# A new order of all steps in a planned block-sparse attention and cosine MLP kernel

## The chip, the cores and the metric

The kernel runs on one core of one Trainium2 chip. The metric is the device time of a launch in microseconds (us), lower is better. A launch was timed in three runs, and one execution was profiled.

## The reference: what is computed

Four batches of eight heads, 768 positions and a head dimension of 64 go through attention with a block mask: blocks of 32, a window of one block to each side, the first and last blocks as rows and columns, and three sampled blocks for each row of blocks. The result, 3072 tokens of 512 values, goes through an MLP with a cosine gate.

```python
scores = scale * np.matmul(q, k.transpose(0, 1, 3, 2))
mask = np.abs(blk_i - blk_j) <= window
mask = mask | (blk_i == 0) | (blk_j == 0) | (blk_i == n_blocks - 1) | (blk_j == n_blocks - 1)
... sampled blocks are set in mask
attn = softmax(np.where(mask, scores, -1e9))
x = np.matmul(attn, v), heads side by side, (3072, 512)
h = x @ w_in                     # (3072, 2048), weights in float64
out = (h * np.cos(h)) @ w_out    # (3072, 512)
```

## The kernel before, in words

Values are split into a high and a low float16 half, so each product is three matmuls. The work is cut into **tiles** of 128 query rows. A batch has five sparse tiles (numbers 0 to 4, then 6 to 10 and so on) and one dense tile with the first and last blocks (5, 11, 17, 23), 24 in all. A sparse tile is worked in four **units** of two heads over 352 gathered keys, a dense one in eight units of one head over 768 keys, 112 units in all.

A unit goes through these steps, named in the planner as given in brackets: scores on TensorE (`qk`, lines 1509 to 1540) into the one scores buffer `sp`; mask and maximum on VectorE (`mx`, 1553); exponential on ScalarE (`ex`, 1575); cast to float16 (`ph`, ScalarE, 1585) and the rest by subtraction (`pl`, VectorE, 1589) into one of three `ring` buffers; a transposing transfer from SP's queue (`PT`, 1604) into one of three `PT` buffers; and the product with the values on TensorE (`pv`, 1614, 1626, 1640) into `xp`. After the last unit the tile is normalised (1653 to 1666) and its output transposed by another transfer (`xT`, 1669). Values come from a scratch tensor into one of two `V` buffers: plain loads from SP (`vg`, 1478 to 1486) and four indirect gathers by GpSimd (`vi`, 1492). One of these two buffers holds the sampled indices and constants at first. Keys are split per batch, transposed into the one `W` (1360) and gathered into `Wg` (1366).

Two tiles make one **feed-forward** pass, 12 in all, each of four chunks of 512 inner columns: four up blocks of 12 matmuls (`m`, 1801), copied out by ScalarE (1810), then rounding, cosine, products and split on VectorE and ScalarE (1820 to 1842), and four down blocks of 6 matmuls (`d`, 1851). Four `g` buffers and two `hs` buffers carry the chunks. At the start 32 float64 weight chunks are loaded (`wl`, 1704), converted with integer operations on VectorE (1712 to 1716), scaled and split; the last eight of them land in `g` buffers.

The order is worked out by a planner before anything is issued. `plan_kernel` (line 523) lists 3193 steps with an engine, a cost, a position, and the buffers read, written and taken. `Plan.run` (398) simulates the engines and repeatedly issues the step that can begin first; among those within `DELTA` = 0.038 us the one of lowest position. Buffers of a class are handed out in the order of the positions of their first steps. The result is one fixed sequence per engine; each engine works it through in order, waiting where data are late. A transfer from SP is modelled as one queue, `dma_free` (lines 492 to 502): it begins 0.65 us after an issue time `hw` or when the queue is free, lasts its `dma` figure (1.73 us for a probability transpose with `hw` 0.63), and counts as landed `DMA_DONE` = 1.15 us later. GpSimd's gathers are booked on the same queue for 1.5 us each (504). A position is a formula of some hundred parameters (`PARAMS`) plus up to three entries of a table `NUDGES`, found by the step's name.

Of the kernel before, what the change touches and what calls it, by code (L numbers as in the profile page):

```python
# [56 lines left out]
NUDGES = dict(  # L57
    idx=3.61, sx=-0.42, regs=-2.95, regs0=-8.34, regs0_0=-6.69, regs1=6.82, regs1_0=-17.04, regs2=3.29, regs2_0=-20.5, regs0_1=-6.69, const=-17.11,
    kload=-0.63, kload0=-0.87, kload0_0=-10.62, ksq=9.39, ksq0=-7.31, ksq0_0=-21.27, kload0_1=-7.01, ksq0_1=-41.01, kload0_2=-66.32, ksq0_2=11.5,
    kred=-0.92, kall=1.38, kall0=-31.15, ksc=-0.19, ksc0=-12.07, regs3=21.51, regs3_0=25.08, regs4=9.54, regs4_0=-19.9, regs1_1=-20.28, regs2_1=3.97,  # L60
    regs3_1=-8.55, regs4_1=15.17, vload=9.28, vload0=-15.15, vload0_0=11.52, vsq=-6.11, vsq0=13.32, vsq0_0=4.72, vload0_1=2.59, vsq0_1=-3.92,
    vload0_2=38.86, vsq0_2=14.54, vred=42.82, vred0=3.99, vall=1, vall0=-0.62, vsc=-5.56, vsc0=-4.67, ql=-0.06, ql0=11.94, qsq=-0.33, qsq0=17.87,
    qsc=-3.82, qsc0=1.9, qu=0.12, qnu=-14.73, qnu0=-6.95, qhi=2.68, qlo=2.81, qlo0=1.37, uT=-0.62, uT0=-18.36, up=2.32, up0=11.32, khi=4.75,
    khi0=9.03, klo=14.9, klo0=12.03, kT=-0.1, kT0=-22.55, kT0_2=4.55, kp=4.16, kp0=0.97, kp0_2=2.55, kT0_3=-0.33, kp0_3=6.32, kT0_4=22.41,
    kp0_4=39.57, kT0_5=6.88, kp0_5=4.01, vhi=0.82, vhi0=13.51, vhi0_0=0.77, vlo=6.66, vlo0=-1.79, vlo0_0=32.44, vst=10.44, vst0=38.45, vst0_0=-44.56,
    vhi0_1=-13.35, vlo0_1=34.43, vst0_1=-3.14, vlo0_2=0.6, vst0_2=29, vhi0_3=4.95, vlo0_3=9.17, vst0_3=-0.45, vhi0_4=-0.81, vst0_4=-36.52,
    vhi0_5=3.24, vlo0_5=22.52, vst0_5=5.35, vg=2.22, vg0=-25.12, vg0_0=11.42, vg0_1=3.7, vg0_2=-0.77, vi=-2.42, vi0=-1.84, vi0_0=-2.26, vi0_1=-10.33,
    vi0_2=9.28, vi0_3=23.96, wgd=-0.98, wgd0=-12.88, wga=3.36, wga0=1.25, wl=-2.63, wl0=-13.24, wc=-1.9, wc0=-0.7, wc0_0=8.57, wc0_1=-15.78,
    wc0_2=-17.45, wsq=-0.65, wsq0=-1.13, wl1=6.28, wc1=13.61, wc1_0=9.36, wc1_1=-9.88, wc1_2=-12.47, wsq1=13.17, wl2=-47.49, wl3=-7.45, wc3=3.57,
    wc3_0=1.61, wc3_1=-6.76, wc3_2=-5.03, wsq3=-6.1, wred=-2, wred0=2.15, wall=1.32, wall0=6.84, wsc=-15.18, wsc0=-20.51, whi=-6.02, whi0=1.04,  # L70
    wlo=2.63, wlo0=3.59, whi2=-0.92, wlo2=-0.14, wl4=9.77, wl5=0.82, wc5=-3.55, wc5_0=20.27, wc5_1=-20.07, wc5_2=-5.13, wsq5=28.26, wl6=8.99,
    wl7=-4.71, wc7=-3.29, wc7_0=-4.88, wc7_1=24.05, wc7_2=9.52, wsq7=-27.78, wred4=-0.63, wall4=0.94, wsc4=-5.92, whi4=18.59, wlo4=7.34, whi6=17.59,
    wlo6=6.23, wl8=-23.81, wl9=6.85, wc9=-14.69, wc9_0=-18.76, wc9_1=21.47, wc9_2=-8.03, wsq9=0.29, wl10=-3.72, wl11=14.55, wc11=-15.06, wc11_0=1.46,
    wc11_1=2.59, wc11_2=6.74, wsq11=16.26, wred8=1.1, wall8=-5.89, wsc8=16.58, whi8=31.98, wlo8=-1.44, whi10=-20.53, wlo10=5.79, wl12=4.39,
    wl13=-15.45, wc13=8.94, wc13_0=-0.92, wc13_1=-0.6, wc13_2=-14.42, wsq13=1.15, wl14=-4.43, wc14=-8.3, wc14_0=-6.73, wc14_1=-8.72, wc14_2=5.6,
    wl15=13.82, wc15_0=10.16, wc15_1=-9.19, wc15_2=0.79, wsq15=5.99, wred12=-0.61, wall12=6.43, wsc12=15.17, whi12=3.82, wlo12=0.5, whi14=49.08,
    wlo14=5.47, wl16=13.24, wl17=30.85, wc17=0.85, wc17_0=-17.27, wc17_1=-0.03, wc17_2=1.79, wsq17=-4.22, wl18=22.91, wc18=-4.52, wc18_0=-2.64,
    wc18_1=-4.76, wc18_2=4.91, wsq18=10.95, wl19=7.23, wc19=-4.21, wc19_0=6.85, wc19_2=-10.01, wsq19=2.09, wred16=-8.69, wall16=17.87, wsc16=-24.31,
    whi16=2.21, wlo16=-18.87, whi18=35.39, wlo18=-19.16, wl20=14.49, wl21=-41.89, wc21=5.55, wc21_0=-1.63, wc21_1=-9.78, wc21_2=-18.56, wsq21=-23.09,
    wl22=50.3, wl23=6.87, wc23=-3.56, wc23_0=-24.76, wc23_1=-9.51, wc23_2=-16.68, wsq23=-11.56, wred20=-30.93, wall20=-3.44, wsc20=-0.04,  # L80
    whi20=-15.71, wlo20=-15.74, whi22=-6.83, wlo22=10.13, wl24=-2.43, wc24=6.19, wc24_0=-3.62, wc24_2=-0.46, wsq24=16.72, wl25=5, wc25=-0.46,
    wc25_0=1.55, wc25_1=0.25, wc25_2=-1.23, wsq25=4.27, wl26=11.94, wc26=-8.12, wc26_0=-16.55, wc26_1=-1.96, wc26_2=-11.56, wsq26=7.92, wl27=0.35,
    wc27=-3.37, wc27_0=-5.24, wc27_1=5.68, wc27_2=49.47, wsq27=4.91, wred24=-15.24, wsc24=-0.49, whi24=-4.49, wlo24=-9.29, whi25=1.62, wlo25=19.32,
    whi26=33.15, wlo26=-4.66, wl28=-8.97, wc28=5.55, wc28_0=-0.52, wc28_1=0.13, wsq28=-6.28, wl29=-1.2, wc29=-61.45, wc29_0=5.2, wc29_1=7.84,
    wc29_2=-31.01, wsq29=-38.92, wl30=8.34, wc30=-9.45, wc30_0=12.37, wc30_1=31.8, wc30_2=20.24, wsq30=0.34, wl31=14.98, wc31=-0.21, wc31_0=-6.47,
    wc31_1=5, wc31_2=-2.32, wsq31=26.29, wred28=4.21, wsc28=5.26, whi28=-19.62, wlo28=-6.21, whi30=2, wlo30=0.25, wmax=15.33, ql1=-5.72, qsq1=-14.68,
    qsc1=3.98, qnu1=1.34, qhi1=-47.08, qlo1=-6.38, uT1=-18.81, up1=-3.53, vg1=-17.37, vg1_0=-9.27, vg1_2=0.1, vi1=30.91, vi1_0=0.48, vi1_1=-18.54,
    vi1_2=0.12, vi1_3=0.12, qk=-0.17, qk0=-58.98, qk0_0=0.24, mx=0.27, mx0=-2.49, mx0_0=-21.81, nb=-3.59, nb0=-8.96, nb0_0=2.59, ex=1.35, ex0=-3.07,
    ex0_0=-22.48, ph=-3.63, ph0=-21.88, ph0_0=-4.4, pl=-21.9, pl0=-22.66, pl0_0=-3.74, PT=-0.26, PT0=4.89, PT0_0=-4.28, pv=0.3, pv0_0=-5.56,
    qk0_1=0.86, mx0_1=-11.94, nb0_1=2.39, ex0_1=2.98, ph0_1=-5.55, pl0_1=15.27, PT0_1=-2.63, pv0_1=6.05, qk0_2=7, mx0_2=-13.62, nb0_2=7.03,  # L90
    ph0_2=0.14, pl0_2=-16.04, PT0_2=-3.48, pv0_2=15.14, qk0_3=18.43, mx0_3=-9.04, nb0_3=9.8, ex0_3=-3.71, ph0_3=7.63, pl0_3=-9.05, PT0_3=-7.28,
    pv0_3=-3, rs=-2.94, rs0=-31.95, rr=-6.44, rr0=6.78, no=0.17, no0=-18.12, xh=0.87, xh0=12.96, xl=0.07, xl0=-4.32, xT=-3.02, xT0=12.24, xp=-14.84,
    xp0=4.93, wgd1=-25.62, wga1=-4.93, ql2=3.86, qsq2=0.31, qsc2=-12.49, qu2=10.26, qnu2=7, qhi2=-4.29, qlo2=-24.12, uT2=-4.61, up2=0.35, vg2=-4.52,
    vg2_0=-58.49, vg2_1=-15.91, vg2_2=-6.89, vi2=-7, vi2_0=-17.32, vi2_1=-0.54, vi2_2=-18.18, vi2_3=2.73, qk1=-0.39, qk1_0=-16.06, mx1=-5.68,
    mx1_0=-7.63, nb1=0.27, nb1_0=0.17, ex1=11.47, ex1_0=4.98, ph1=-9.02, ph1_0=0.22, pl1=-6.66, pl1_0=-0.96, PT1=-13.96, PT1_0=-15.61, pv1=10.71,
    pv1_0=-16.09, qk1_1=-4.02, mx1_1=-2.64, nb1_1=-3.56, ex1_1=16.53, ph1_1=-3.84, pl1_1=-6.4, PT1_1=0.59, pv1_1=1.72, qk1_2=-2.71, mx1_2=1.47,
    nb1_2=0.13, ex1_2=11.37, ph1_2=-4.64, pl1_2=-1.25, PT1_2=-4.99, pv1_2=9.69, qk1_3=-1.21, mx1_3=1.13, ex1_3=-6.56, ph1_3=3.94, pl1_3=-2.83,
    PT1_3=2.29, pv1_3=13.9, rs1=-2.68, rr1=5.45, no1=-7.24, xh1=-3.98, xl1=-9.69, xT1=25.61, wgd2=-13.96, wga2=-2.4, m=0.34, m0=7.68, m0_0=-2.33,
    turn=-7.57, turn0=-18.26, turn0_0=1.62, ev=-4.58, ev0=-4.52, ev0_0=-21.06, sce=-7.02, sce0=50.11, ka=5.66, ka0=1.78, ka0_0=-3.5, kb=-1.13,
    kb0=4.68, kb0_0=-13.36, sin=0.46, sin0=-0.93, sin0_0=2.79, gm=1.05, gm0=-7.53, gm0_0=24.9, gh=-2.94, gh0=21.43, gh0_0=-12.51, gl=-17.79,  # L100
    gl0=-5.58, gl0_0=-4.21, turn0_1=5.61, ev0_1=0.45, sce1=1.82, ka0_1=-9.91, kb0_1=-14, sin0_1=1.7, gm0_1=14.55, gh0_1=-7.7, gl0_1=-13.54,
    m0_2=-3.6, turn0_2=-40.38, ev0_2=2.87, sce2=1.57, ka0_2=4.5, kb0_2=-6.01, sin0_2=5.35, gm0_2=1.98, gh0_2=-6.52, gl0_2=11.76, m0_3=-3.22,
    turn0_3=16.55, ev0_3=11.54, sce3=4.59, ka0_3=8.66, kb0_3=3.09, sin0_3=-1.35, gm0_3=16.12, gh0_3=-10.16, gl0_3=-6.97, d0=-3.17, d0_0=-3.86,
    o=1.98, o0=-0.17, o0_0=8.97, o0_1=11.85, d0_1=3.25, d0_2=1.64, d0_3=2.26, st=16.31, st0=-13.05, st0_0=5.76, st0_1=16.22, ql3=14.11, qsq3=10.1,
# [1825 lines left out]
```

## Time and profile before

| | |
|---|---|
| median of 3 runs | 895.02 us (893.42 to 896.33) |
| span of the profiled execution | 851.5 us |
| that execution's own time | not listed |
| instructions in the span | 23033 |
| mean granted TensorE clock | 0.936 |
| TensorE busy with matmuls | 727.7 us, 9272 matmuls |
| VectorE, ScalarE, GpSimd busy | 644.8, 624.8, 101.8 us |

The span runs from the first to the last instruction on the core; the time of a launch also holds what lies around it. Busy times of engines overlap one another. A granted clock of 1.0 is 2.4 GHz and 0.5 is 1.2 GHz. "DMA" is the mean busy share of the core's 16 transfer engines; it can pass 1.0 where packets of two queues overlap.

### The profile page before, as it was taken

The page shows a single profiled execution, that of the slowest core. Times are in us where ns is not written, and L with a number is a line of the kernel's source. Part 1 is how long each engine was busy: PE and PEld are TensorE (multiplying, and loading weights), DVE is VectorE, ACT ScalarE, POOL GpSimd, SP SyncE. Part 2 cuts the span into 40 slices and gives each one's busy share as a digit, 9 for nine tenths or more (in the row PEclk, how much of TensorE's full clock was granted, in tenths as well). Part 3 has the DMA queues.
Part 4 walks back from the last instruction along what each step waited for, and adds up shares of the span by engine and source line. Part 5 has one row for each costly group of instructions (what it writes and reads, how often), then busy time and mean ns, then how long its engine had stood idle before and what let it go on. Part 6 is the DMA issues. An engine that isn't in the chain of part 4 may idle for free.

```text
span 851.5 us, 23033 instructions
## 1 busy us (share of the span) xinstructions
PE 727.7 (85%) x9272; PEld 506.8 (60%) x9272; DVE 644.8 (76%) x1632; ACT 624.8 (73%) x1193; POOL 101.8 (12%) x128
## 2 busy tenths in 40 slices
PE   3556667779999869987999979999988869999997
PEld 2444554546767537656767548677665548576583
DVE  3999989998967776878668876879578746867352
ACT  1686846888867898788758978779669857769342
POOL 5211231000030101200020111000020111000000
PEclk9965697879999979999999999999999989999999
DMA  9999893398895989899979999989696997855300
GB/s 253 324 208 275 211 264 98 73 233 166 213 222 127 201 164 194 157 230 149 228 159 182 196 177 170 216 133 165 191 156 116 184 196 155 181 83 118 87 2 25
DMA packets 313306, 146.54 MB, mean 172 GB/s; under 512 B 266224, under 2 KB 290928, under 8 KB 313200
## 3 DMA queue, kind: packets, MB, share of 16 engines
q1 hardware_dynamic: 308080, 129.35, 73.1%
q0 software_dynamic: 5120, 15.73, 8.4%
q8 instruction: 72, 1.18, 0.6%
q14 instruction: 34, 0.28, 0.1%
HBM read 68.23 MB, written 12.58 MB: 95 GB/s over the span
## 4 chain that ended last, share of the span: by engine, by line
PE 40%; ACT 12%; DMA 11%; DVE 10%; issue 3%; SPq 1%; DVEq 0%; ACTq 0%
PE ph L1801 19%; PE po L1851 15%; DMA PT<-ring 6%; ACT P L1575 4%; DVE P L1553 3%; DMA W<-kn 2%; DMA xT<-n 2%; ACT ring L1585 2%; DVE ring L1589 1%; PE xp L1640 1%; PE xp L1626 1%; PE sp L1520 1%; DVE hs L1833 1%; DVE g L1842 1%; DVE g L1824 1%
## 5 line engine op out<-in xcount | busy, mean ns | idle before, releaser
L1801 PE MATMUL ph<-xT,w 128*128 128x256 f16 x2304 | 270.8, 278 | 10.1 <-DMA xT<-n 6.7
L1851 PE MATMUL po<-w,g 128*128 128x512 f16 x1152 | 269.0, 383 | 8.6 <-ACT g L1839 7.1
L1801 PEld LDWEIGHTS <-w 128*128 128x128 f16 x2304 | 226.5, 99 | 47.6 <-issue 7.3
L1851 PEld LDWEIGHTS <-g 128*128 128x128 f16 x1152 | 108.2, 98 | 128.0 <-ACT g L1839 7.4
L1575 ACT ACTIVATE P<-P,sm 128x352 f32<-128x352 f32 (+1 forms) x224 | 151.9, 679 | 28.8 <-DVE sm L1570 19.3
L1492 POOL DMA_INDIRECT V<-scr,gidx x80 | 89.2, 1115 | 613.4 <-PE xp L1614 316.0
L1589 DVE TENSOR_TENSOR ring<-P,ring 128x704 f16<-128x704 f32 (+1 forms) x112 | 100.1, 906 | 31.5 <-ACT ring L1585 30.1
L1810 ACT ACTIVATE hs<-ph,sm 128x512 f32<-128x512 f32 x96 | 64.4, 680 | 50.8 <-PE ph L1801 42.8
L1585 ACT CAST ring<-P 128x704 f16<-128x704 f32 (+1 forms) x112 | 86.5, 785 | 13.0 <-DMA PT<-ring 11.9
L1553 DVE CUSTOM_DVE_ANT_1 P<-sp,bias 128x352 f32<-128x352 f32 x160 | 77.7, 518 | 14.1 <-PE sp L1526 13.1
L1833 DVE SCALAR_TENSOR_TENSOR hs<-hs,sm,g 128x1024 f32<-128x1024 f32 x48 | 61.0, 1281 | 23.6 <-ACT g L1828 22.4
L1520 PE MATMUL sp<-W,U 128*128 128x192 f16 x320 | 53.2, 268 | 29.2 <-DVE sm L1553 27.7
L1828 ACT ACTIVATE g<-g,sm 128x1024 f32<-128x1024 f32 x48 | 54.7, 1146 | 23.7 <-DVE g L1824 23.4
L1842 DVE TENSOR_TENSOR g<-hs,g 128x1024 f16<-128x1024 f32 x48 | 58.6, 1223 | 17.1 <-ACT g L1839 16.9
L1839 ACT ACTIVATE g<-hs 128x1024 f16<-128x1024 f32 x48 | 50.4, 1051 | 18.2 <-DVE hs L1833 17.5
L1824 DVE SCALAR_TENSOR_TENSOR g<-g,hs 128x1024 f32<-128x1024 f32 x48 | 58.3, 1220 | 0.5
L1521 PEld LDWEIGHTS <-U 128*128 128x128 f16 x320 | 33.4, 104 | 35.7 <-issue 32.0
L1614 PE MATMUL xp<-V,PT 96*32 96x64 f16 x1920 | 31.0, 202 | 22.0 <-DMA PT<-ring 18.8
L1820 DVE TENSOR_SCALAR g<-hs 128x1024 f32<-128x1024 f32 x48 | 32.9, 691 | 21.8 <-ACT hs L1810 20.1
L1521 PE MATMUL sp<-W,U 128*128 128x64 f16 x320 | 48.7, 207 | 0.0
L1626 PE MATMUL xp<-V,PT 128*128 128x64 f16 x960 | 45.5, 201 | 0.0
L1614 PEld LDWEIGHTS <-PT 96*32 96x32 f16 x1920 | 21.6, 102 | 37.7 <-DMA PT<-ring 25.9
(176 smaller groups left out, 896.0 us busy)
## 6 DMA issues: line engine op xcount, KB each, us to landing
V<-scr SPq DMA_DIRECT2D x20, 384.0 KB
stage<-in_k_dram SPq DMA_DIRECT2D x12, 512.0 KB
w<-in_moe_w_in_dram SPq DMA_DIRECT2D x12, 512.0 KB
w<-in_moe_w_out_dram SPq DMA_DIRECT2D x12, 512.0 KB
V<-scr SPq DMA_DIRECT2D x8, 768.0 KB
scr<-n SPq DMA_DIRECT2D x21, 256.0 KB
qs<-in_q_dram SPq DMA_DIRECT2D x20, 256.0 KB
U<-U SPq DMA_DIRECT2D x40, 128.0 KB
```

Of the source, the lines that this page charges most:

```text
L1492: self.nc.gpsimd.indirect_dma_start(V[:96, 2 + j, :], None, self.scr[b][:, :], bass.IndirectOffsetOnAxis(ap=self.gidx[:96, c : c + 1], axi ...
L1521: mm(spv[:, :, 96:128].rearrange("p y (n c) -> p y n c", c=hf), u, ends, start=False, stop=False)
L1553: self.nc.vector.tensor_tensor_reduce(out=self.p_view(n, Pt)[:, a].rearrange("p (n c) -> p n c", c=hf), in0=sp[:, :w].rearrange("p (n c) - ...
L1575: self.nc.scalar.activation(Pv[:, a], Pv[:, a], AF.Exp, scale=qc[:, 4:5], bias=nb[:, bcol : bcol + 1], accum_out=sums[:, 2 * j + a : 2 * j ...
L1585: self.nc.scalar.copy(R[:, :, 0, : self.width(n)], self.p_view(n, Pt))
L1589: self.nc.vector.tensor_tensor(R[:, :, 1, :w], self.p_view(n, Pt), R[:, :, 0, :w], ALU.subtract)
L1801: self.nc.tensor.matmul(ph[:, ff, :], self.W1[p][:, wl, cc, c * P : (c + 1) * P], xT[:, xl * NCC + cc, :], start=(j == 0), stop=(j == len( ...
L1810: self.nc.scalar.activation(hs[:, h * 512 : h * 512 + 512], ph.rearrange("p f t -> p (f t)"), AF.Copy, scale=self.turns[b][:, p : p + 1])
L1824: self.nc.vector.scalar_tensor_tensor(kt, kt, MAGIC, hs, op0=ALU.subtract, op1=ALU.subtract)
L1833: self.nc.vector.scalar_tensor_tensor(hs, hs, c[:, p : p + 1], kt, op0=ALU.mult, op1=ALU.mult)
L1842: self.nc.vector.tensor_tensor(g[:, 1024:2048], hs, g[:, 0:1024], ALU.subtract)
L1851: self.nc.tensor.matmul(po, g[:, gl, ff, t * P : (t + 1) * P], self.W2[p][:, wl, ff, :], start=(first and ff == half * hf and j == 0), sto ...
```

## The change

`NUDGES` is removed. A list `POS` of 3193 numbers takes its place, and each step's position is the entry with its own number, whatever the formula gave. The planner's model of transfers is changed: SP's queue and GpSimd's queue each have an end of their own, transfers that overlap run at half speed while they do, the figure of an SP transfer is multiplied by 1.1, a gather takes 1.1 us, and landing comes 1.3 us after the end. `PARAMS`, the steps and their engines, and every function that issues an instruction stay.

```diff
-NUDGES = dict(
-    idx=3.61, sx=-0.42, regs=-2.95, regs0=-8.34, regs0_0=-6.69, regs1=6.82, regs1_0=-17.04, regs2=3.29, regs2_0=-20.5, regs0_1=-6.69, const=-17.11,
...
+POS = [
+    -532.03, -810.177, 89.397, -131.085, -65.302, -89.144, -544.854, -540.202, -322.968, -385.34, -105.865, -127.653, -505.194, -345.924, -499.035,
...
-DMA_DONE = 1.15
+DMA_DONE = 1.3
+DMA_SLOW = 1.1
+POOL_DMA = 1.1
...
+class Queues:
+    def __init__(self):
+        self.ends = [0.0, 0.0]
+
+    def run(self, which, at, work):
+        other = self.ends[1 - which]
+        begin = max(at, self.ends[which])
+        if other <= begin:
+            end = begin + work
+        else:
+            shared = other - begin
+            end = begin + 2 * work if work <= shared * 0.5 else begin + shared + (work - shared * 0.5)
+            self.ends[1 - which] += (min(end, other) - begin) * 0.5
+        self.ends[which] = end
+        return end
...
-        for key in nudge_keys(name):
-            o.pos += NUDGES.get(key, 0.0)
+        if len(self.ops) < len(POS):
+            o.pos = POS[len(self.ops)]
...
-                dma_free = d + o.dma
-                o.done = dma_free + DMA_DONE + o.lat
+                o.done = dma.run(0, h + 0.65, o.dma * DMA_SLOW) + DMA_DONE + o.lat
             elif o.dma:
-                dma_free = max(o.end + 1.0, dma_free) + o.dma
-                o.done = dma_free + DMA_DONE + o.lat
+                o.done = dma.run(1, o.end + 1.0, POOL_DMA) + DMA_DONE + o.lat
```

Because buffers are handed out by position, the two lists of positions give the order in which steps take them. The scores buffer, `xp`, `Wg`, `qs` and `P` go out in the same order but for the key and value maxima of one batch; the others change among neighbours:

| buffer | before | after |
|---|---|---|
| `V`, first four | index tile, tile 0, tile 2, tile 1 | index tile, tile 1, tile 0, tile 2 |
| `g`, weight chunks | 24, 27, 28, 25, 29, 26, two of pass 0, 30, 31 | 31, 25, 24, 29, 27, 26, 28, one of pass 0, 30 |
| `ring`, tiles 7 to 9 | 7_0 7_1 7_2 8_0 7_3 8_1 9_0 8_2 8_3 9_1 | 7_0 7_1 7_2 7_3 8_0 8_1 8_2 8_3 9_0 9_2 |
| `ring`, tiles 14 to 17 | 14_0 14_1 15_1 14_2 15_2 15_0 14_3 16_0 15_3 16_1 16_2 17_0 16_3 | 14_0 14_1 14_3 14_2 15_0 15_3 15_2 15_1 16_1 16_0 16_2 16_3 17_0 |
| `ring`, tiles 19 to 23 | 20_1 ahead of 19_3; 22_3 ahead of 23_0 | 19_3 ahead of tile 20; 23_0 ahead of 22_3 |

## Rows read from the trace of the kernel before

**Rows 1.** The page's line of engines: busy us, share of the span, instructions.

```profile
PE 727.7 (85%) x9272; PEld 506.8 (60%) x9272; DVE 644.8 (76%) x1632; ACT 624.8 (73%) x1193; POOL 101.8 (12%) x128
```

**Rows 2.** The page's 40 slices of the span: busy tenths of TensorE and VectorE, granted clock, transfer engines.

```profile
PE   3556667779999869987999979999988869999997
...
DVE  3999989998967776878668876879578746867352
...
PEclk9965697879999979999999999999999989999999
DMA  9999893398895989899979999989696997855300
```

**Rows 3.** The windows view, one row for a stretch from start to end in us: its length, then busy us (and instructions) of TensorE, its weight loads, VectorE, ScalarE, GpSimd; granted clock, share of the transfer engines, GB/s.

```profile
25.00:225.00 200.00, 143.23 (x2036) 105.14 (x2033) 187.83 (x481) 151.09 (x293) 28.46 (x20) 0.80 0.84 203
225.00:850.00 625.00, 576.49 (x7173) 395.32 (x7173) 446.90 (x1107) 466.67 (x891) 60.71 (x60) 0.98 0.81 159
270.00:330.00 60.00, 48.09 (x861) 29.69 (x858) 46.64 (x159) 52.93 (x121) 8.25 (x8) 0.91 0.97 186
620.00:700.00 80.00, 63.59 (x944) 39.78 (x942) 58.89 (x184) 60.46 (x133) 11.41 (x13) 0.95 0.93 160
675.00:700.00 25.00, 18.46 (x315) 11.22 (x313) 15.64 (x59) 18.57 (x47) 3.67 (x4) 0.90 1.07 185
805.00:851.50 46.50, 42.11 (x290) 28.15 (x288) 17.15 (x16) 16.02 (x19) 0.00 (x0) 1.00 0.06 19
50.00:80.00 30.00, 16.92 (x388) 13.30 (x388) 27.35 (x83) 21.36 (x50) 4.06 (x4) 0.67 1.10 241
```

**Rows 4.** The list of waits, TensorE's matmuls alone, from 225 to 850 us: line that waited, engine and line waited for, us in total, times, longest.

```profile
PE sp L1520 <- DVE sm L1553: 15.5, 15, 2.7
PE xp L1614 <- DMA PT<-ring: 11.0, 11, 2.5
PE po L1851 <- ACT g L1839: 7.1, 2, 5.4
PE ph L1801 <- DMA xT<-n: 5.3, 3, 3.2
PE xp L1640 <- DMA PT<-ring: 2.4, 2, 2.1
PE po L1851 <- DVE g L1842: 1.5, 3, 0.7
PE sp L1537 <- DVE sm L1553: 1.5, 1, 1.5
PE ph L1801 <- ACT hs L1810: 1.0, 1, 1.0
PE sp L1526 <- ACT Wg L1366: 0.4, 1, 0.4
```

**Rows 5.** The chain of work that ended last: its shares by line, then of its longest pieces (start, us, what) the first and the last of ten probability transposes, and the up blocks of the tail.

```profile
by line: PE ph L1801 19.0%; PE po L1851 15.2%; DMA PT<-ring 6.3%; ACT P L1575 4.0%; issue 3.3%; DVE P L1553 2.6%; DMA W<-kn 2.1%; DMA xT<-n 2.1%; ACT ring L1585 1.9%; DVE ring L1589 1.4%; PE xp L1640 1.3%; PE xp L1626 1.2%; PE sp L1520 1.1%
...
220.87 5.42 DMA PT<-ring
...
680.03 5.33 DMA PT<-ring
...
805.43 20.96 PE ph L1801 x192
```

**Rows 6.** GpSimd's gathers: the page's group (count, busy us, mean ns of one, idle before), its transfer queue's share of 16 engines' span, and, of the values tile, the us from a gather's issue to its landing.

```profile
L1492 POOL DMA_INDIRECT V<-scr,gidx x80 | 89.2, 1115 | 613.4 <-PE xp L1614 316.0
...
q0 software_dynamic: 5120, 15.73, 8.4%
...
DMA to landing us min/median/max: 3.1/5.8/11.5
```

**Rows 7.** The timeline from 684 to 700 us, SP's issue of an output transpose, then two starts of TensorE: start us, us, engine, line, operation, count, and in brackets the idle us before it and what ended them.

```profile
689.98 2.59 SPq L1669 DMA_TRANSPOSE xT<-n  x1
...
694.18 0.36 PE L1614 MATMUL xp<-V,PT 96*32 96x64 f16 x24 [2.53 <-DMA PT<-ring]
...
698.20 2.08 PE L1801 MATMUL ph<-xT,w 128*128 128x256 f16 x9 [3.20 <-DMA xT<-n]
```

**Rows 8.** The list of waits, VectorE's alone, from 25 to 225 us: those for weights.

```profile
DVE stage L1712 <- DMA w<-in_moe_w_in_dram: 2.2, 1, 2.2
DVE w L1712 <- DMA w<-in_moe_w_out_dram: 1.8, 2, 1.0
...
DVE w L1712 <- DMA w<-in_moe_w_in_dram: 0.7, 1, 0.7
```

**Rows 9.** The timeline: the first gathers of tile 0 and of tile 1 on GpSimd, and the first products of tiles 0 and 1 with their values.

```profile
35.50 1.45 POOL L1492 DMA_INDIRECT V<-scr,gidx  x1 [16.44 <-DMA w<-in_moe_w_out_dram]
...
54.62 0.53 PE L1614 MATMUL xp<-V,PT 96*32 96x64 f16 x24
...
65.34 0.92 POOL L1492 DMA_INDIRECT V<-scr,gidx  x1 [19.28 <-PE xp L1614]
...
79.41 0.53 PE L1614 MATMUL xp<-V,PT 96*32 96x64 f16 x24
```

**Rows 10.** The page's groups of the cast and the subtraction of a unit's probabilities: count, busy us, mean ns of one, idle before.

```profile
L1589 DVE TENSOR_TENSOR ring<-P,ring 128x704 f16<-128x704 f32 (+1 forms) x112 | 100.1, 906 | 31.5 <-ACT ring L1585 30.1
...
L1585 ACT CAST ring<-P 128x704 f16<-128x704 f32 (+1 forms) x112 | 86.5, 785 | 13.0 <-DMA PT<-ring 11.9
```

More of the change, by code (lines that the diff above doesn't have):

```diff
@@ L307 @@
+POS = [
[199 rows of a table added]
+]
 LAT = dict(PE=0.2, ACT=0.145, DVE=0.13, POOL=0.09, SP=0.0)
-DMA_DONE = 1.15
+DMA_DONE = 1.3
+DMA_SLOW = 1.1
+POOL_DMA = 1.1
 TABLE_LOAD = 1.41
@@ L417, in run @@
         free = dict.fromkeys(ready, 0.6)
-        dma_free, table, order, clock = 0.0, None, [], ArrayClock()
+        dma, table, order, clock = Queues(), None, [], ArrayClock()
         def ready_now(o):
@@ L444, in run @@
             for eng, cand in ready.items():
-                at = max(free[eng], dma_free - 1.75) if eng == "SP" else free[eng]
+                at = max(free[eng], dma.ends[0] - 1.75) if eng == "SP" else free[eng]
                 lim, times = 1e18, []
@@ L493, in run @@
                 h = t + o.hw
-                d = max(h + 0.65, dma_free)
+                d = max(h + 0.65, dma.ends[0])
                 if o.hw != 0.63:
```

246 lines of the change are left out of this document (removed), and 198 rows, old and new, of the table POS.

## The prediction, made before the change was run

> **What bounds the kernel now.** I read the page's engine line first: TensorE is busy 727.7 of 851.5 us, so 124 us of it stand idle, and no other engine comes near [rows 1]. The slices of the page say where. In the first ten the matmul engine is at 3 to 9 tenths and VectorE at 9; later TensorE is at 9 with dips, and the transfers are at 7 to 9 nearly all along [rows 2]. Cut into stages: from 25 to 225 us VectorE is busy 187.83 of 200 us, so the start is bound by VectorE; from 225 to 850 TensorE is busy 576.49 of 625 us, so 48.5 us are idle, and much of that lies in stretches such as 270 to 330 (11.9 us) and 620 to 700 (16.4 us) [rows 3]. From 805 us on TensorE runs without a gap until the last store. The list of TensorE's waits after 225 us names 45.7 of the 48.5 us: 17.0 for VectorE's read of the one scores buffer (15.5 and 1.5), 13.4 for the transposed probabilities (11.0 and 2.4), 5.3 for the transposed attention output, 10.0 for the feed-forward chain and the gathered keys [rows 4]. The chain that ended last says the same: transposes of probabilities are 6.3% of it, those of outputs and keys 2.1% each [rows 5].
>
> The profiled execution's own time is not listed. Its span is 851.5; I put it at the median of the three runs, 895.0, so 43.5 us lie around the span and do not change. A gain in the span is a gain in the time.
>
> **The change part by part.** Nothing is computed otherwise: the step functions and the switches that choose an engine stay, so the 9272 matmuls, 80 gathers and every transfer remain. What moves is the place of each of the 3193 steps. Sorting the steps that take a buffer by old and new position shows that the structure stays too: scores units, tiles and feed-forward blocks come in the same sequence but for neighbours. So the sum consists of waits, not of work.
>
> *Transfers priced later.* In the old planner a probability transpose comes due 0.63 + 0.65 + 1.73 + 1.15 = 4.16 us after its issue, behind gathers booked at 1.5 us each on the same queue; in the new one 0.63 + 0.65 + 1.90 + 1.3 = 4.48 us, and longer while a gather runs beside it. In the chain the first and last listed take 5.42 and 5.33 us [rows 5]. The shortfall of 5.4 - 4.16 = 1.24 us falls to 0.92: a quarter is mended for a lone transpose. Beside a gather the shared stretch is doubled, up to 1.1 us more, which mends all of it. The gathers' queue held 8.4% of 851.5 us, 0.89 us for each of 80 [rows 6], so 1.1 on a queue of its own is nearer than 1.5 on the common one. The waits this speaks to are 13.4 + 5.3 = 18.7 us after 225 us [rows 4]. Bounds: a quarter, 4.7, to all, 18.7; I take half, 9.3, as transposes beside gathers are about as common as lone ones. With a transfer expected later, TensorE does an up or down block first (12 up matmuls 1.31 us, from 20.96 us for 192 in the tail [rows 5]); late next is the scores step behind that block, which is the rival below.
>
> One slice says how far this can go. At 689.98 an output transpose is issued, and the up block that needs it starts at 698.20, 8.2 us later, after a wait of 3.20 us; another of 2.53 us for probabilities stands just before [rows 7]. The transfer engines' share is 1.07 in that slice [rows 3]: it is queueing, not price. The Trainium skill says in "DMA: Bandwidth & Descriptors", section "Issuing engines are not separate DMA queues", that transfers started by different engines run on the same 16 engines and interleave. By that rule two planned queues add no throughput and these 6.3 us would stay; the sum would lose half of that, 3.1, and come to 886. By the rows alone I leave them in: the new order may also issue the transpose ahead of what it queued behind.
>
> *Start.* From 25 to 225 us VectorE is idle 12.2 us; its waits for weights are 2.2, 1.8 and less [rows 8]. The new order loads weight chunk 31 into a feed-forward buffer ahead of chunks 25, 24, 29, 27, 26 and 28, though its conversion comes last: one buffer of four is parked. Bounds: 12.2 gained, 2.2 lost (one more such wait). I take half of the two largest waits, 2.0 gained.
>
> *Values of tile 1 before tile 0.* The free value buffer now goes to tile 1; its four gathers, at 65.34 us now, go ahead of tile 0's, which start at 35.50 [rows 9]. Four times 1.12 us plus gaps of 0.3 puts tile 0's back by 5.7 us; its last gather would end about 47 and land 5.8 us later [rows 6], near 52, while its product starts at 54.62. Hidden by the first probability transpose, with 2 us of cover; if it goes, those land on a stretch bound by VectorE (27.35 of 30 us busy [rows 3]). Tile 1's product, at 79.41, could start earlier, behind the same VectorE work. Taken as 0, bounds 2 either way.
>
> *Order within tiles.* By the old positions a later tile's unit got its probability buffer ahead of the earlier tile's last at six tile borders (7/8, 8/9, 14/15, 15/16, 16/17, 19/20); by the new ones at one (22/23). Each turn is worth one cast and one subtraction, 0.79 + 0.91 = 1.69 us [rows 10]: the earlier tile's output comes that much sooner, the later tile's first unit that much later. On the path only where the output transpose is waited for, already counted. Taken as 0, bounds five times 1.69, 8.5, either way.
>
> *Turns of engines.* The other 27.0 us of waits after 225 us (45.7 - 18.7) end on VectorE or ScalarE. Every step of these was re-placed, and no row says which way it goes: 0, bounds half of it either way, 13.5.
>
> *SP's and GpSimd's queues.* All 434 transfers of SP and the 80 gathers keep their instructions. SP is a queue that waits in order, so a transfer placed ahead of its data holds all behind it; this cost sits in the transpose waits above.
>
> Sum: 9.3 + 2.0 = 11.3 us off 895.0, about 883.5; I say 883.
>
> **The rivals.** *More comes off (chance 0.18).* From 225 to 850 us the granted clock is 0.98, so 0.02 x 2 x 625 = 25 us ran at 1.2 GHz, and it fell where waits are: 0.90 at 675 to 700, 1.00 in the tail [rows 3]. Work at half speed costs up to 12.5 us more than at 2.4 GHz. If all 18.7 us of transfer waits go, 18.7 / 45.7 of it, 5.1 us, come back too; with 2 from the start that is 25.8 us, 869. The Trainium skill ("TensorE: Matmul & The Clock Gate", section "HAM oscillation — how this bites in real kernels") describes transfer waits that throttle the array and make the next work start slow; the 0.90 beside the 3.20 us wait agrees. Against: the waits in crowded slices.
>
> *Slower (0.24).* Transfers expected later make the planner put up and down blocks into the gap, ahead of a scores step. There is one scores buffer, and VectorE and ScalarE take turns on each unit, so a block of 1.31 us ahead delays the unit, its transpose and the tile's output. The place is the dense tiles at the end of each batch: 24 units after 225 us. If half get one block more, 12 x 1.31 = 15.7 us are lost, less a quarter of the transfer waits gained, 4.7: 11 us, 906. It decides from 7 such units on, where 7 x 1.31 eats the 9.3. For it: the largest wait is already the scores buffer's, 15.5 us in 15 waits [rows 4]. Against: TensorE works through the same total, so a block done early is gone later.
>
> *No difference (0.13).* Transfers at a share of 0.81 after 225 us [rows 3] and 1.07 in places are near full, and what one tile gains the next gives back, or the new positions, whatever their number, issue nearly the present order. Then the time is 895. For it: only neighbours change places in the buffer orders.
>
> **How the numbers follow.** The forecast, 883, has 0.45; its own range is 873 to 892 (the quarter and the whole of the 18.7 with the start's terms). A measurement of this kernel can tell about 0.3%, 2.7 us. Faster: 0.45 + 0.18 = 0.63; same 0.13; slower 0.24. The range has to reach both neighbours: down to 866, just under the 869, and up to 906, the slower case; about 0.07 lies below and 0.12 above.
>
> **What the profile after would show.** If right: TensorE's busy time and the bytes moved as before; in the waits after 225 us those for the two transposes together down from 18.7 us to 10 or less, those on the scores buffer near 17; 620 to 700 us, or where its batch border then lies, with fewer idle us; VectorE still above 185 of 200 us at the start. The larger gain shows as a clock of 0.99 or more after 225 us. I am wrong if the transpose waits stay and the gain comes from VectorE's turns or the start, or if waits on the scores buffer grow by more than 9 us.

## The result and the profile after

The changed kernel takes **862.3 us** (median of 4 runs, 859.73 to 868.48) where the kernel before, run beside it, takes 894.2 (888.55 to 896.33): ratio 0.9662, 95% interval 0.9609 to 0.9714. It is 32 us faster; 12 were forecast, and 862.3 lies under the range's lower end of 866. The sign was right, the size was not. Ratios in this document leave out single disturbed executions, so one can differ from the quotient of the medians.

The page of the changed kernel, profiled in an execution that took 864.64 us: the span, busy us of each engine, then the busy tenths of TensorE and VectorE, the granted clock and the transfer engines in 40 slices.

```profile
span 862.6 us, 23031 instructions
...
PE 736.8 (85%) x9272; PEld 511.6 (59%) x9272; DVE 643.7 (75%) x1632; ACT 629.0 (73%) x1197; POOL 101.4 (12%) x128
...
PE   3526669479999988999989979999889899999998
...
DVE  3958999998885976788938866786868777767443
...
PEclk9956579689999979999998999999999999999999
DMA  9999979079899899895995999898993998646400
```

Two things are to be seen. The span is 2.0 us under the execution's own time. And this span, 862.6, is *longer* than the one of the kernel before in the profile that the prediction rests on, 851.5. Set against [rows 1, 2], the change seems to make the kernel slower by 11 us, while the timed runs say 32 us faster. The two profiles are not of one kind of execution, as the waits show. TensorE's waits from 225 to 850 us in the changed kernel follow (line that waited, engine and line waited for, us in total, times, longest). The same code has other line numbers in each kernel: 1586, 1598 and 1612 are the products with the values (1614, 1626 and 1640 before), 1492 and 1498 scores (1520, 1526), 1773 the up blocks (1801) and 1823 the down blocks (1851). `ph` is what an up block writes and `po` what a down block writes.

```profile
PE ph L1773 <- issue: 7.1, 10, 1.1
PE sp L1492 <- DVE sm L1525: 7.0, 5, 3.2
PE xp L1586 <- issue: 5.0, 10, 0.8
PE xp L1598 <- issue: 4.5, 8, 1.2
PE xp L1612 <- DMA PT<-ring: 2.7, 3, 1.1
PE sp L1498 <- issue: 2.7, 1, 2.7
...
PE xp L1586 <- DMA PT<-ring: 2.2, 3, 0.9
...
PE ph L1773 <- DMA xT<-n: 0.9, 1, 0.9
```

The transposes and the scores buffer, the heads of [rows 4], have shrunk; but 19.3 us are new, put down to "issue", which is idle time that no wait in the trace explains. [Rows 4] has none of it.

### The profile page after: what moved, and what is told of

It reads as the page before. It is cut to its first block, busy times and chain, and to the rows that moved or that the text cites. A ratio compares the mean times of both kernels' runs of the same rounds, so it can differ in the third digit from the quotient of the medians.

```text
span 862.6 us, 23031 instructions
## 1 busy us (share of the span) xinstructions
PE 736.8 (85%) x9272; PEld 511.6 (59%) x9272; DVE 643.7 (75%) x1632; ACT 629.0 (73%) x1197; POOL 101.4 (12%) x128
## 3 DMA queue, kind: packets, MB, share of 16 engines
q1 hardware_dynamic: 308080, 129.35, 74.9%
q8 instruction: 72, 1.18, 0.6%
## 4 chain that ended last, share of the span: by engine, by line
PE 51%; DVE 17%; DMA 11%; issue 10%; ACT 6%; another core or an unknown queue 2%; POOL 1%; SPq 1%; DVEq 0%; ACTq 0%; POOLq 0%
PE ph L1773 20%; PE po L1823 20%; DMA PT<-ring 3%; DVE P L1525 3%; PE xp L1598 2%; DMA xT<-n 2%; PE sp L1492 2%; DMA w<-in_moe_w_in_dram 2%; PE sp L1509 2%; PE xp L1586 2%; PE xp L1612 2%; DMA w<-in_moe_w_out_dram 1%; ACT P L1547 1%; PE sp L1498 1%
## 5 line engine op out<-in xcount | busy, mean ns | idle before, releaser
L1823 PE MATMUL po<-w,g 128*128 128x512 f16 x1152 | 274.6, 389 | 5.4 <-DVE g L1814 4.6
L1805 DVE SCALAR_TENSOR_TENSOR hs<-hs,sm,g 128x1024 f32<-128x1024 f32 x48 | 61.4, 1282 | 13.4 <-ACT g L1800 13.1
L1800 ACT ACTIVATE g<-g,sm 128x1024 f32<-128x1024 f32 x48 | 54.8, 1147 | 20.5 <-DVE g L1796 20.1
L1811 ACT ACTIVATE g<-hs 128x1024 f16<-128x1024 f32 x48 | 50.4, 1051 | 15.9 <-DVE hs L1805 15.7
L1586 PE MATMUL xp<-V,PT 96*32 96x64 f16 x1920 | 33.1, 200 | 19.8 <-DMA PT<-ring 11.8
```

Of the source, the lines that this page charges most:

```text
L1586: mm(xp[32 * j : 32 * j + 32, h, :], PT[:96, 6 * a + 3 * l + 2, 32 * j : 32 * j + 32], V[:96, 2 + j, h, d0:d1], start=(a == 0 and x == 0), ...
L1823: self.nc.tensor.matmul(po, g[:, gl, ff, t * P : (t + 1) * P], self.W2[p][:, wl, ff, :], start=(first and ff == half * hf and j == 0), sto ...
```

## One program, two levels of time

The unchanged programs ran in six sessions; each of the last five was on one chip:

| session | before, us | after, us | ratio |
|---|---|---|---|
| the timed runs | 894.2 | 862.3 | 0.9662 |
| first | 857.0 | 846.4 | 0.9865 [0.9829, 0.9902] |
| second | 855.8 | 849.2 | 0.9859 [0.9797, 0.9921] |
| third | 900.7 | not run | |
| fourth | 859.0 | 844.3 | 0.9838 [0.9776, 0.9901] |
| fifth | 895.2 | 868.5 | 0.9672 [0.9548, 0.9796] |

In three sessions the kernel before takes 856 to 859 us and the change gives 1.4 to 1.6%; in three it takes 894 to 901, and where the change ran there it gives 3.3 to 3.4%. Comparisons below go by ratios. The first run of the study settles what lies around the span.

**e1_before**: the kernel before, unchanged.

> The kernel before, unchanged, to get the span of its timed executions: the profile shown of it has a span of 851.5 us while its runs take 888.6 to 896.3, and the kernel after has a span only 2 us under its time. Theory A (the time lies inside): its executions here have spans of 886 to 894 us, 2 us under their times, and the trace shows 35 to 43 us more of waiting at transfers than the profile shown. Theory B (the time lies around): a span near 851 and a time near 894.

Measured 858.76 us, ratio 1.0023 [0.9992, 1.0053], and a span of 856.1 in an execution of 858.37: **2.3 us lie around the span, not 43.5**. Theory A is right in that, but its 886 to 894 us did not come, as the kernel before takes 857.0 us in the first session. So the profile of before, with its span of 851.5, is of an execution of about 854 us, of the quicker kind, while the three runs shown were of the longer kind.

The same two programs, profiled in the fourth session (quicker) and the fifth (longer):

> The kernel before, unchanged, as the measure for the three beside it. Chips differ: its median was 857 and 856 us on two of them and 901 on a third. If this one is of the third kind, Theory I (TensorE is short of work handed to it there) expects the 40 us more to stand as idle time of TensorE that nothing in the trace ends, or that ends with an unknown releaser, above 30 us, and waits for transfers within 10 us of those of the quick chips. Theory D (data transfers are slower there) expects waits for weights and transposes 20 us or more above the quick chips' 22 us. On a quick chip it expects 855 to 860 us and tells neither.

> The changed kernel, unchanged. Ratio to the kernel before 0.986 on a chip where that takes 857 us, 0.960 to 0.970 on one where it takes 900. The measure for the next kernel.

> The kernel before, unchanged, for its trace. On a chip of the quick kind (855 to 860 us) it tells nothing new. On a chip of the kind on which it takes about 900 us, Theory I (TensorE is short of work handed to it) expects TensorE's idle time without a releaser, and waits on an unknown releaser, above 30 us, with TensorE's busy time also up by 10 us or more at the same 9272 matmuls; Theory D (slower data transfers) expects the waits for weights and transposes 20 us or more above the quick chips'.

> The changed kernel, unchanged: ratio 0.984 to 0.987 to the kernel before on a quick chip, 0.960 to 0.970 on the other kind.

f1_before took 859.1 us, f2_after 844.3, g1_before 898.7, g2_after 868.5. TensorE's waits from 225 to 850 us, first in f1_before:

```profile
PE sp L1520 <- DVE sm L1553: 15.0, 15, 2.9
PE xp L1614 <- DMA PT<-ring: 9.6, 14, 1.7
PE po L1851 <- ACT g L1839: 7.8, 2, 5.8
PE ph L1801 <- DMA xT<-n: 6.8, 3, 3.6
PE sp L1537 <- DVE sm L1553: 1.7, 1, 1.7
PE po L1851 <- DVE g L1842: 1.5, 3, 0.7
```

These repeat [rows 4] within 3 us. The changed kernel in the same session, f2_after:

```profile
PE xp L1586 <- DMA PT<-ring: 8.0, 8, 1.8
PE sp L1492 <- DVE sm L1525: 6.4, 7, 1.2
PE xp L1612 <- DMA PT<-ring: 2.3, 3, 1.1
...
PE ph L1773 <- ACT hs L1782: 1.9, 3, 1.0
...
PE po L1823 <- DVE g L1814: 1.2, 1, 1.2
...
PE po L1823 <- ACT g L1811: 0.8, 1, 0.8
...
PE ph L1773 <- DMA xT<-n: 0.4, 1, 0.4
```

And the kernel before in the fifth session, g1_before:

```profile
PE sp L1520 <- DVE sm L1553: 22.2, 16, 5.0
PE ph L1801 <- ACT hs L1810: 13.2, 3, 6.3
PE xp L1614 <- issue: 8.6, 12, 1.2
PE xp L1614 <- DMA PT<-ring: 6.0, 8, 1.1
PE po L1851 <- ACT g L1839: 5.9, 2, 5.0
...
PE ph L1801 <- DMA xT<-n: 2.5, 2, 2.0
```

Grouped by what was waited for, and closed so that the terms of each pair make up the difference of the spans:

| us | f1 before | f2 after | change | g1 before | g2 after | change |
|---|---|---|---|---|---|---|
| span | 851.8 | 837.2 | -14.6 | 899.0 | 866.9 | -32.1 |
| probabilities' transposes | 10.6 | 10.3 | -0.3 | 7.4 | 6.8 | -0.6 |
| outputs' transposes | 6.8 | 0.4 | -6.4 | 2.5 | 2.0 | -0.5 |
| scores buffer (`sp`, on VectorE) | 16.7 | 8.0 | -8.7 | 24.1 | 10.5 | -13.6 |
| down blocks (`po`, on `g`) | 9.3 | 2.3 | -7.0 | 7.6 | 2.5 | -5.1 |
| `ph` on `hs`, issue, others | 1.2 | 8.3 | +7.1 | 26.6 | 24.3 | -2.3 |
| idle elsewhere, mostly the start | 79.7 | 85.0 | +5.3 | 87.4 | 84.7 | -2.7 |
| TensorE busy, 9272 matmuls | 727.5 | 722.9 | -4.6 | 743.4 | 736.1 | -7.3 |

So in these traces the longer session costs the old order 47.2 us and the new one 29.7, and that difference of 17.5 us is about what the timed runs show beyond 1.6%. On TensorE it is made up of `hs`, issue and others (9.4), idle time elsewhere (8.0), the scores buffer (4.9) and busy time (2.7), less 7.5 at the transposes and the down blocks. In f1 and f2, and in every other trace of a quicker session, no wait has an unknown releaser ("remote"). In g1 the readers of TensorE's results have 13 such waits, 52.8 us in all; in g2 there are 11, 36.5 us, and every other trace of a longer session has 10 to 13. The largest groups, VectorE and ScalarE of g1_before:

```profile
DVE P L1553 <- remote: 31.6, 9, 5.3
ACT hs L1810 <- remote: 21.2, 4, 7.3
```

and of g2_after:

```profile
DVE P L1525 <- remote: 18.6, 6, 4.9
ACT hs L1782 <- remote: 13.5, 3, 5.5
```

What one such stretch looks like, in the timeline of g1_before (start, duration, engine, line, operation; in brackets the idle time just before and its releaser):

```profile
375.65 3.58 PE L1851 MATMUL po<-w,g 128*128 128x512 f16 x9
...
379.60 0.35 PE L1526 MATMUL sp<-Wg,U 128*32 128x96 f16 x16
...
380.01 0.53 DVE L1553 CUSTOM_DVE_ANT_1 P<-sp,bias 128x352 f32<-128x352 f32 x1 [6.19 <-PE sp L1526]
...
380.43 1.46 PE L1851 MATMUL po<-w,g 128*128 128x512 f16 x6
```

Nine down matmuls take 3.58 us, 0.40 each, and six shortly after take 1.46, 0.24 each; VectorE stands 6.19 us for the scores behind them. The windows of this stretch give the granted clock (ahead of the transfer engines' share):

```profile
375.00:379.00 4.00, 4.00 (x12) 1.40 (x10) 0.00 (x0) 0.56 (x2) 0.00 (x0) 0.55 1.03 228
379.00:382.00 3.00, 3.00 (x73) 2.07 (x71) 1.80 (x6) 0.71 (x3) 0.00 (x0) 1.00 0.61 102
```

0.55 is nearly all at 1.2 GHz. Over the whole run TensorE is busy 743.4 us instead of 727.5 for the same matmuls. The expectations called I (TensorE short of work handed to it) and D (slower data transfers) divide. D asked for 20 us *more* waiting for weights and transposes, but the two transposes fell from 17.4 to 9.9 us, and VectorE's waits for weights from 25 to 225 us went from 4.1 to 4.6. The page's line of the hardware queue agrees: `q1 hardware_dynamic: 308080, 129.35, 73.2%` of 851.8 us in f1 and `q1 hardware_dynamic: 308080, 129.35, 68.6%` of 899.0 in g1 are 624 and 617 us for the same packets. I asked for over 30 us of unexplained waits and 10 of busy time; there are 18.9 us of "issue" in the whole run, 52.8 of unknown releasers and 15.9 of busy time. That the stops are at TensorE and at the readers of its results, and not in the data transfers, is shown by this. That TensorE lacks work handed to it fits the signs but is not shown, and what delays it is open: the instruction queue's line is the same but for its share, `q8 instruction: 72, 1.18, 0.6%` in f1 and `q8 instruction: 72, 1.18, 0.5%` in g1. Nor is it shown that it belongs to a chip: the first and the fifth session were on chips of the same number, at 857 and 895 us.

## The other experiments

Two theories were open for the gain itself: that it comes from the planner's new picture of transfers (as forecast), or from the list of positions, which re-places every step and so also the turns of the engines.

**e2_oldpos_newmodel**: the kernel before with the new model of transfers alone. **e3_newpos_oldmodel**: the changed kernel with the old model.

```diff
 (e2, in the kernel before)        (e3, in the changed kernel)
-DMA_DONE = 1.15                   -DMA_DONE = 1.3
+DMA_DONE = 1.3, class Queues ...  +DMA_DONE = 1.15, dma_free ...
```

> The old positions (formula and NUDGES) run through the new planner with its two transfer queues. Theory M (the transfer model makes the gain, by the prediction's first term): at least half of the 32 us, 878 or less. Theory P (the positions, searched one by one, make it): 888 to 905, as the old positions were fitted to the old model.

> The new list of positions run through the old planner with its one transfer queue. Theory M: the gain is lost, 885 to 905. Theory P: most of it stays, 862 to 875.

Measured 892.6 us, ratio 1.0365 [1.0283, 1.0448], and 917.5, ratio 1.0712 [1.0657, 1.0767], in the session where before takes 857.0. Neither half carries the gain: each alone loses, and 917.5 is outside what either theory expected of e3. The waits for transposes after 225 us grow to 38.4 and 45.9 us, against 20.0 in e1_before. The planner takes whatever can begin first, so a change of a few tenths of a microsecond in a transfer's price can lead to another sequence; that each list of positions fits the model that it was found with is how I read the two losses, and the step at which the sequences part was not looked for. The new model alone did not give fewer waits for transfers: in e2 they take nearly twice as long.

**e4_after, e5_after**: the changed kernel, unchanged, in the first two sessions.

> The kernel after, unchanged, beside the others on one chip. Theory A: 858 to 868 with a span 2 us less; both orders are then compared at the same speed of transfers.

> The kernel after once more, for a trace of an execution at the full clock and for the scatter between executions and chips. Theory S (same conditions, small gain): 1.0 to 1.6% under the kernel before, as on the chip of the last call (0.9865), with waits of TensorE's matmuls on the two kinds of transposes after 225 us at 10 us or less and those on the scores buffer under 10. Theory C (the chip decides): where the kernel before takes 888 to 896 us the gain is 3 to 4%, where it takes 857 it is 1 to 1.6%.

846.4 and 849.2 us, ratios 0.9865 and 0.9859: about 12 us where before takes 857, close to the forecast sum of 11.3. That sum took the right total from the wrong terms, as the table shows, so the agreement is luck.

Theory S expected 10 us or less for the two kinds of transposes and under 10 for the scores buffer. The second came, the first did not, in the trace of e5_after (an execution of 849.84 us, one of the longer of its six):

```profile
PE xp L1586 <- DMA PT<-ring: 13.8, 8, 3.7
PE sp L1492 <- DVE sm L1525: 6.3, 7, 1.3
PE xp L1612 <- DMA PT<-ring: 3.1, 5, 1.1
...
PE ph L1773 <- DMA xT<-n: 0.8, 1, 0.8
```

The transposes take 17.7 us here, 16.9 of them for probabilities, where the kernel before has 10.6 to 13.4 for these in its three quick traces; f3_tile1_values_later, below, has 17.3. So, with one order behind the start, the waits for probabilities scatter from trace to trace by several us. The scores buffer (7.5 us) and the down blocks (2.3) repeat f2_after.

**e6_new_start, e7_old_start, e9_new_from_batch2, f4_old_start, g3_old_start**: the two orders joined. The planner's result is replaced by a fixed list, one order up to a point and the other behind it.

```diff
-    pl.run(PARAMS["DELTA"], PARAMS["TSTICK"], PARAMS["MSTICK"])
+    for n in ORDER:      # e6: new order to tile 6's first scores, then old
+        ...              # e7, f4, g3: old, then new; e9: old through batch 1
-        for o in pl.order:
-            o.fn()
+        for n in ORDER:
+            pl.ops[n].fn()
```

> The new order up to the first scores step of batch 1 (1068 steps, tile 6, near 257 us of the plan), the old order from there on, both fixed as lists with the buffers that each planner gave. By the prediction (most of it after the start): 2 us under the kernel before, 853 to 857 where that takes 857. Rival (the start holds the gain): 9 us or more under it.

> The old order up to the first scores step of batch 1 (1063 steps), the new order from there on. By the prediction: 9 us under the kernel before, about 848 where that takes 857. Rival (the start holds the gain): within 3 us of the kernel before. The two parts' gains should add to that of the whole change within 4 us if the parts don't lean on each other.

> The old order up to the first scores step of batch 2 (1769 steps), the new order from there on. New from batch 1 on gave 15 to 17 us. Theory D (many small turns everywhere): two thirds of that, 9 to 12 us under the kernel before. Theory O (one place in batch 1): 4 us or less under it.

> The old order up to tile 6's scores, then the new one. On a quick chip 0.981 of the kernel before, as found; that is 4 to 5 us under the changed kernel. On a chip where the kernel before takes 900 us: if what it loses there lies behind the start, it stays 4 or more us under the changed kernel (ratio to before 0.955 to 0.965); if it lies in the start, it comes out above the changed kernel, at 0.975 or more.

> The old order up to tile 6's scores, then the new. It was 10 us under the changed kernel on one chip and 1 us on another. If the new start loses: 5 us or more under the changed kernel here, ratio to before 0.980 or less on a quick chip. If it does not: within 3 us of it.

| run | us | ratio to before | ratio of the whole change there |
|---|---|---|---|
| e6_new_start, second session | 872.7 | 1.0167 [1.0109, 1.0225] | 0.9859 |
| e7_old_start, second | 839.0 | 0.9813 [0.9767, 0.9858] | 0.9859 |
| f4_old_start, fourth | 843.4 | 0.9839 [0.9767, 0.9911] | 0.9838 |
| g3_old_start, fifth | 870.1 | 0.9757 [0.9671, 0.9842] | 0.9672 |
| e9_new_from_batch2, third | 885.7 | 0.9855 [0.9794, 0.9916] | not run; 0.966 to 0.967 in sessions like it |

With the old start the new order behind it gives the whole gain of the quicker sessions; the new start alone, with the old order behind it, loses 1.7%. So on those the gain comes from behind the start. After e6 and e7 I held that the new start costs time. f4 and g3 took that back: against the changed kernel beside it the old start is 0.46% ahead (4 us), level, and 0.85% behind (8 us), with intervals of about half a per cent or more on each. In f4_old_start TensorE's idle time outside the listed waits is 5.0 us less than in f2_after (80.0 against 85.0), but it is busy 4.6 us more (727.5 against 722.9), and the two cancel. The parts of e6 and e7 don't add up to the whole either (+1.7 and -1.9% against -1.4%), so e6 measures a bad joint besides the start. In the longer sessions e9 keeps somewhat under half of the gain, 13 us: by the ratios of other sessions, part of it there comes from the first two batches.

**e8_tile1_values_later, f3_tile1_values_later**: the new order with the seven transfers of tile 1's values put, in the list of steps, behind the last product of tile 0 (the edit in words; in the kernel it is the list `ORDER`).

```diff
+# vg1_*, vi1_* taken out of ORDER and put in again behind pv0_3
```

> The new order with one thing changed: the seven transfers of tile 1's values (three plain loads, four gathers) stand behind the last product of tile 0, as in the old order, and tile 0's go first. In the new order's trace VectorE waits 7.2 us at 61 us for weight chunk 9, which was issued at 48.5, and a probability transpose's product waits 6.4. Theory Q (the transfers of both tiles' values at 35 to 50 us crowd out the weights): that wait is under 2 us and the kernel is 5 us or more faster than the new order, 844 or less where that takes 849. Theory W (the weight loads' own order does it): the wait and the time stay within 3 us.

> The new order with the seven transfers of tile 1's values moved behind tile 0's. Theory Q: these transfers ahead of tile 0's are what the new start loses by, through the weight chunk that came 7.2 us late; 8 to 14 us under the changed kernel beside it, ratio to it 0.984 to 0.991. Rival S: the new start loses by its order of steps as a whole and the late chunk only takes the place of other waits: within 4 us of the changed kernel.

In the changed kernel VectorE stands 7.1 us for one weight chunk in a stretch that the prediction called covered. VectorE's waits for weights from 25 to 225 us in f2_after, and the end of the longest in the timeline:

```profile
DVE w L1684 <- DMA w<-in_moe_w_in_dram: 9.6, 2, 7.1
...
DVE w L1684 <- DMA w<-in_moe_w_out_dram: 2.2, 1, 2.2
```

```profile
60.98 0.69 DVE L1684 TENSOR_SCALAR w<-w 128x1024 int32<-128x1024 int32 x1 [7.14 <-DMA w<-in_moe_w_in_dram]
```

In f3 only three of the seven moved in time: tile 1's plain loads, issued by SP from 69.76 us on instead of from 34.13 in f2. GpSimd has nothing to wait for before tile 1's four gathers, so they run where they ran, only behind tile 0's now. The last of the eight gathers in f3:

```profile
44.91 0.92 POOL L1414 DMA_INDIRECT V<-scr,gidx  x1 [0.30 <-issue]
```

Eight gathers stand there in the old order too (from 36.20 us in f1, for tiles 0 and 2). So the two runs test the three loads and an exchange of the gathers, and do not take tile 1's values out of the stretch.

VectorE's waits for weights fall from 11.8 to 8.3 us in f3, but VectorE then has one wait of 7.8 us for TensorE's scores:

```profile
DVE P L1475 <- PE sp L1448: 8.3, 3, 7.8
DVE w L1634 <- DMA w<-in_moe_w_in_dram: 5.2, 2, 4.1
DVE w L1634 <- DMA w<-in_moe_w_out_dram: 3.1, 2, 2.3
```

f3 took 850.6 us, ratio to before 0.9864 [0.9781, 0.9948], beside 0.9838 for the changed kernel. Theory Q expected 0.984 to 0.991 of that, 0.968 to 0.975, which lies under the interval. e8, in the third session, gave 860.5 us and 0.9529 [0.9468, 0.9590], better than the 0.966 to 0.967 of the changed kernel in sessions like it, with weight waits of 4.8 us where g2_after has 10.9. The two signs don't agree, and Theory Q is neither held up nor refuted: the late chunk is real, and its price on the path was not shown.

**e10_old_late, e11_new_late**: one more transfer of 32 KB on SP's queue ahead of each of the 108 probability transposes, in both kernels.

```diff
     def p_transpose(self, R, PT):
+        self.nc.sync.dma_start(self.pad[self.pads], self.ident)
+        self.pads += 1
```

> The kernel before with an extra transfer of 32 KB to a scratch tensor ahead of each of its probability transposes on SP's queue, 108 in all; it makes each transpose later by the extra's issue, 0.3 to 0.6 us, and fills the transfer engines a little more. Theory L (the old order suffers more when transfers come late, and that is why the runs with 888 to 896 differ by 4% from its other runs while the new order's differ by 2%): 25 to 45 us slower than the kernel before. Theory E (both suffer alike): the same loss as the new order's within 5 us.

> The new order with the same extra transfers. Theory L: a loss against the new order of at most two thirds of the old order's loss, so 5 to 20 us. Theory E: the same loss as the old order's within 5 us, so the new order stays 1.2% ahead.

The question was whether the old order loses more in the longer sessions because its transfers have less slack. e10 took 906.7 us, ratio 1.0055 [1.0016, 1.0094]; e11 873.9, ratio 0.9727 [0.9663, 0.9791], against 0.9672 for the changed kernel without the extra transfers, in another session. The old order loses 0.55%, about 5 us, where Theory L asked for 25 to 45. The new one loses as much if the fifth session's ratio held in the third; with an interval of 1.2% on that ratio it can't be told from zero. Their waits for probabilities from 225 to 850 us, of e10_old_late:

```profile
PE xp L1617 <- DMA PT<-ring: 11.6, 14, 2.5
...
PE xp L1643 <- DMA PT<-ring: 3.6, 3, 2.0
```

and of e11_new_late:

```profile
PE xp L1589 <- DMA PT<-ring: 11.6, 8, 3.0
PE xp L1615 <- DMA PT<-ring: 8.9, 7, 2.1
```

From 7.4 to 15.2 us in the old order, from 6.8 to 20.5 in the new: late transfers lengthen these waits no less in the new order, which was planned with late transfers. Theory L falls, by e10 alone.

## Why the prediction was right or wrong

**The base: wrong, and this is the step that failed.** "43.5 us lie around the span and do not change" came from setting one profile beside runs of another level. In every run of this study 2 us lie around the span. The profile was of a kernel at about 854 us; at that level the forecast sum of 11.3 us is 1.3%, and the change gave 1.4 to 1.6% (0.9865, 0.9859, 0.9838). The runs to be forecast stood 40 us higher, in stretches that the profile does not have, and about half of the 32 us came off those (the change is worth 14.6 us in the quick pair of traces and 32.1 in the longer). No row of [rows 1 to 10] could price them; that an unlisted time stood 43.5 us off the span could have been read as a sign that the profile was of another kind of run, and it should have widened the range downward. The forecast's own range of 873 to 892 does not come out of its terms either: 18.7 + 2.0 off 895 is 874, and with the start's bound of 12.2 it is 864.

**Transfers priced later: 9.3 forecast, 6.7 found in one pair of traces, from the other transfer.** The bounds of 4.7 and 18.7 held in that quicker session (17.4 to 10.7), but not in e5_after, with 17.7 where the kernel before has 17.4 to 20.0, and the reasoning did not hold. The shortfall per probability transpose, 1.24 us against 0.92, was its core, and the probability transposes' waits did not move: 10.6 and 10.3 us. In e5_after they are longer, 16.9. All of the gain came from output transposes, 6.8 to 0.4 us. In the longer session hardly anything was there to gain, 9.9 to 8.8. e2 shows that the new model alone makes such waits worse, not better.

The rule weighed there, from the Trainium skill's "DMA: Bandwidth & Descriptors", section "Issuing engines are not separate DMA queues", would have left the crowded slice's waits in. The sum's size by that rule, 6.2 for this term, is nearer to 6.7 than the rows' 9.3, but the wait it spoke for is gone: the longest wait for an output transpose, 3.20 us in [rows 7], is 0.4 us in f2_after and 0.8 in e5_after. The measurement decides for the rows: an order can take a wait out of a crowded slice at the same bytes. The share of 1.07 was weak ground for "queueing": from 5 to 22 us of the kernel before, ahead of the first gather, the share is 1.17, so it passes 1.0 without a second queue of data.

**Turns of engines: booked 0, and the largest term.** The waits on the scores buffer fall by 8.7 us and those of the down blocks by 7.0, together 15.7 in the quicker session and 18.7 in the longer. The bound of 13.5 was too narrow, as it let half of the 27.0 us move. Against it stand 7.1 us of new waits in the quicker session, for `hs`, issue, gathered values and others. "No row says which way it goes" was true; that such a term is zero does not follow.

**Start: booked 2.0 gained, loss bound 2.2.** VectorE is busy 177 us of 200 where over 185 were expected, with weight waits of 11.8 us where [rows 8] has 2.2 and less:

```profile
25.00:225.00 200.00, 136.53 (x1963) 101.81 (x1962) 177.11 (x454) 148.08 (x282) 22.55 (x20) 0.78 0.86 193
```

TensorE's idle time outside the listed waits is up by 5.3 us, so, counted in idle time, the term had the wrong sign and passed its bound; the joined orders leave its net price between 4 us lost and 8 gained.

**Values of tile 1 before tile 0: booked 0, bounds 2.** Tile 0's last gather ends at 46.40 us in f2_after, as forecast (about 47), but tile 0's first product starts at 59.75 instead of 54.70, after 6.69 us put down to its probability transpose, so the cover of 2 us was not what decided there. f3 gave nothing that can be told from zero, but it left tile 1's gathers in place: whether the term is 0 stays open.

**Order within tiles** was not tried by itself, and its 0 stays open.

**The rivals.** *More comes off* named the direction. A price through the clock fits: from 225 to 835 us the granted clock is 0.97 in f1_before and 0.99 in f2_after, and TensorE is busy 4.6 us less; in the longer pair 7.3, where 5.1 had been put on it. It was not isolated: f4_old_start has 0.99 there as well and is busy 727.5 us, as long as f1_before. The rule beside it, from the Trainium skill's "TensorE: Matmul & The Clock Gate", section "HAM oscillation — how this bites in real kernels", agrees with that sign. Its mechanism, all 18.7 us of transfer waits gone, was not what happened. *Slower* needed scores-buffer waits over 9 us longer; they are 8.7 shorter, so units delayed by blocks in the gaps are not what this order does. The prediction's own sign of being wrong was that "the transpose waits stay and the gain comes from VectorE's turns or the start": those for probabilities stayed, those for outputs went, and the larger part of the gain came from VectorE's turns.

What stays open: what holds TensorE up in the longer sessions, and why the old order loses 17.5 us more by it. The unexplained waits of the readers, 52.8 us in g1_before and 36.5 in g2_after, differ by about that much, but they are idle time of VectorE and ScalarE, and the changed kernel's trace of the timed runs has 13 of them with 41.0 us. No run changed the stops alone.

## What to carry to other kernels

Before a sum is made, set the span of the profile against its own time; if the timed runs stand far off, the profile is of another level, and the forecast needs either a range that reaches to it or a ratio in place of microseconds. A re-planned order moves waits of every kind, so the terms that nothing names (the turns of engines) deserve a size as large as the waits that they touch, with either sign. A list of positions and the model that it was found with are one thing: swapping either alone cost 3.7 and 7.1% here. And look in the trace whether a moved step moved in time: an engine with nothing to wait for runs it where it ran before.

## What was not expected of the hardware

One program took 856 to 859 us in some sessions and 894 to 901 in others, with 727.5 and 743.4 us of TensorE's busy time for the same 9272 matmuls. In the longer ones TensorE's matmuls and the readers of its results stop for 1.3 to 7.3 us with no known releaser, 13 times in g1_before and in no trace of a quicker session, and such a stop can be followed by work at a granted clock near 0.5 (0.55 from 375 to 379 us). The kernel's data transfers show no such difference: the hardware queue's packets take 617 us there against 624, and the waits for transposes are shorter.
